# A fused attention and feed-forward kernel on one core: the last batch's norm writes token order, and the last output tile is summed in two column pieces

## The chip, the cores and the metric

The kernel runs on one core of one Trainium2 chip. The metric is the device time of one execution in microseconds (us), the median of several runs. The engines are named as the profile names them: PE is the matrix engine (PEld its weight loads), DVE the vector engine, ACT the scalar engine, POOL the GpSimd engine and SP the engine that here only issues DMAs. "hT", "A", "o" and the like are names of tiles in the program; "L601" is line 601 of the kernel.

## The reference, cut to what matters

```python
# q, k, v: (8 batches, 8 heads, 576 tokens, 64); p: (8, 8, 32, 64), all float32
def sm_attn(qq, kk, vv):
    s = scale * np.matmul(qq, kk.transpose(0, 1, 3, 2))      # scale = 1/8
    a = np.exp(s - np.max(s, axis=-1, keepdims=True))
    a = a / (np.sum(a, axis=-1, keepdims=True) + 1e-09)
    return np.matmul(a, vv)
p_packed = sm_attn(p, k, v)                # 32 packed rows per head
out = sm_attn(q, p_packed, p_packed)       # (8, 8, 576, 64)
x = out.transpose(0, 2, 1, 3).reshape(4608, 512)
h = x @ w_in                               # (4608, 2048)
g = np.where(h >= 1, h, np.where(h <= -1, 0.0, (h + 1) ** 2 / 4))
return g @ w_out                           # (4608, 512) float32
```

## The kernel before

**Tiling.** The work goes batch by batch, 8 batches of 576 tokens. For a batch, K and Q are turned so that the head dimension lies on the partitions, the packed attention gives `ppT`, and two things follow from it: `M = ppT · w_in` (the packed rows already sent through the first weights; 128 partitions by 2 head groups `g` by 2048), and the second softmax `A` (128 partitions by 2 groups `g`, two halves `x` of 288 tokens each). `A` is made by a chain: exponentials `eT` on ACT, their sums `sm` on PE, `ln` and `rc = exp(-ln)` on ACT, and then `norm` (L473) on DVE, which multiplies `eT` by the packed rows' reciprocal `rs` and by `rc`. There are two norms for a batch, one for each group.

**Hidden tiles.** `hidden_tile` makes one of 16 blocks `fi` of 128 hidden units of a batch: four matmuls (L549: group 0 with halves 0 and 1, then group 1 with halves 0 and 1) into a PSUM tile `h`, then `x` on ACT (L554), a second step on DVE or ACT (L559, L561) and a third on DVE (L564) that writes the block into `hT`. With `M` and `A` both in, the block needs all four halves of `A`.

**Output tiles.** Two batches make a pair of 1152 token columns in `hT`, and nine output tiles of 128 columns each. `out_tile` sums 16 matmuls (L601) of 512 columns in a PSUM tile `o`, copies it to `ob` (L320 is the line of the copying helper, on ACT or DVE), and SP issues the DMAs that write the rows to the output. Token columns don't stand in the order of the output's rows: half `x` holds three stretches `e` of 96 columns, and column `t` of stretch `e` is row `6t + 2e + x` of the batch. So a tile's rows are written in pieces that end at each 96th column, two for most tiles. In the last pair, tiles 0 to 3 need batch 6 alone, tile 4 both, and tiles 5 to 8 batch 7.

**The last tile** (pair 3, tile 8) is summed in two halves of 256 columns, one in `o`, one in a PSUM tile `o2` of the pool `psW`. For each `fi` PE runs both halves, one after the other. At the end ACT copies columns 0 to 255 and issues two DMAs of its own (96 and 32 rows), DVE copies columns 256 to 511, and SP issues two DMAs for these.

**What sets the order.** Everything is given to a planner (`Plan`) as tasks with dependencies, keys and costs `C[...]`; it simulates the engines and writes each engine's instructions in the order in which it would start them. A changed cost can therefore move instructions on PE, ACT and DVE. PE's instruction stream takes an output matmul wherever the hidden tiles leave room. The DMAs of ACT and SP count their landing in eight counters, DMAHW0 to DMAHW7, which DMAs take in turn; a DMA waits for the one before it on its counter. Behind the program's last instruction SP waits for all of the counters, one after the other, in the order of their numbers (the instructions at L702).

Of the kernel before, what the change touches and what calls it, by code (L numbers as in the profile page):

```python
# [8 lines left out]

C = dict(load=3.5666, half=1.46, w_in=2.57, w_out=2.57, rest=1.25, out=9, p=4.05, land=2.0125, xt=6.5, xland=11, tpp=0.06, tp=0.042, sc=0.034, pk=0.9765, s2=0.2862, sm=0.245, M=0.2415, h=0.49, o=0.217, switch=0.05, join=0.1604, pTc=0.1, Tca=1.12, Tcd=0.76, ex=0.82, ppT=0.42, ppo=0.41, ppa=0.4, ppd=0.2, rs=0.18, eT=0.74, ln=0.65, rc=0.68, A=0.82, Mca=1, Mcd=1.22, x=0.65, ta=0.683, td=0.489, hT=0.758, oba=0.585, obd=0.6276, array=0.2, wake=1.2, warm=4.2, early=0.3, tell=0.034, feed=0.085, slack=0.51, margin=0.1717, wait=0.5)
NW, NO, NX, NB = 3, 2, 5, 6
DW, FILL = 256, 512
TURNED = 3


# [164 lines left out]
def kernel(  # L182
# [10 lines left out]
    nc = tc.nc  # L193
# [44 lines left out]
    def wide(shape, dtype, name):  # L238
        return psW.tile(shape, dtype, tag="w", name=name)
# [61 lines left out]
    add_weights("in", 0)  # L301
    add_weights("in", 1)
    add_weights("out", 0)
    add_weights("in", 2)
    add_weights("out", 1)
    add_weights("in", 3)
    add_weights("out", 2)
    add_load("k", 1, 2)
    add_load("v", 1, 1)
    add_load("q", 1, 2)  # L310
    add_weights("out", 3)
    L["p"] = add(DMA, C["rest"], -1, (), lambda: nc.gpsimd.dma_start(p_nat[:, PB * 2:], p_v[:, PB * 2:]))


# [4 lines left out]
    def copy(out_, in_):  # L319
        return lambda eng: nc.vector.tensor_copy(out_, in_) if eng == DVE else nc.scalar.copy(out_, in_)  # L320
# [37 lines left out]
    def attention(b, key):  # L358
# [85 lines left out]
        def weights(g, deps, r):  # L444
# [25 lines left out]
                nc.scalar.activation(box["rc"], box["ln"], AF.Exp, scale=-1.0)  # L470

            def norm(eng):
                nc.vector.scalar_tensor_tensor(A()[:, g], box["eT"], rs()[:, g, :1], box["rc"], ALU.mult, ALU.mult)  # L473
            p_ = K.get((b - 1, "A" + str(g)), [])
            t, j = yield ky, C["s2"], deps + p_, mm
# [50 lines left out]
        pk, pc, r = zip(*([packed((0,), [e0]), packed((1,), [e1])] if b == 0 else [packed((0, 1), [e0, e1])] * G))  # L526
# [58 lines left out]
    def out_tile(pr, i):  # L585
        box, prev = {}, []
        bs = range(2 * pr + i * P // S, 2 * pr + ((i + 1) * P - 1) // S + 1)

        end = 2 * pr + 2 == B and i + 1 == NT

        cuts = [12, KF] if pr == 0 and i < 4 else [KF]
        w = d_model // 2

        def spare():
            box["o2"] = wide([P, w], f32, "o2")

        def step(fi):
            if fi == 0 or fi in cuts:
                box["o"] = psO.tile([P, d_model], f32, tag="o", name="o")
            for o, cs in [(box["o"][:, :w], slice(w)), (box["o2"], slice(w, d_model))] if end else [(box["o"], slice(d_model))]:  # L600
                nc.tensor.matmul(o, hT[:, fi, i * P:(i + 1) * P], w_out_sb[:, fi, cs], start=(fi == 0 or fi in cuts), stop=(fi + 1 in cuts))  # L601

        def kept(eng):
            box["part"] = att.tile([P, d_model], f32, tag="part", name="part", bufs=4)
            copy(box["part"], box["o"])(eng)

        def done(eng):
            box["ob"] = ops.tile([P, d_model], f32, tag="ob", name="ob")
            if len(cuts) > 1:
                nc.vector.tensor_tensor(box["ob"], box["o"], box["part"], ALU.add)  # L610
            else:
                copy(box["ob"], box["o"])(eng)
            for a, n, dst in out_rows(pr, i):
                nc.sync.dma_start(dst, box["ob"][a:a + n])

        def done_last(eng):

            for j, (eng, queue, o) in enumerate(((ACT, nc.scalar, box["o"][:, :w]), (DVE, nc.sync, box["o2"]))):
                ob = ops.tile([P, w], f32, tag="ob" + str(j), name="ob" + str(j), bufs=1)
                copy(ob, o)(eng)  # L620
                for a, n, dst in sorted(out_rows(pr, i), key=lambda x: -x[1]):
                    queue.dma_start(dst[:, j * w:(j + 1) * w], ob[a:a + n])
        if end:
            prev = [add(PE, 0.0, 100 + pr * NT + i, [K[B - 1, "h"][-1]], spare, takes="W", readers=1)]
        for fi in range(KF):
            t = add(PE, C["o"], 100 + pr * NT + i, [wrote[b, fi] for b in bs] + prev + [L["out", fi // 4]],
                    lambda fi=fi: step(fi), mode=0, takes="O" if fi == 0 or fi in cuts else None, readers=1, slack=C["slack"])
            step_of[pr, i, fi] = t
            prev = [t]
            if fi == 0 or fi in cuts:  # L630
                owner = t
            if fi + 1 in cuts[:-1]:
                first = both(kept, C["oba"], C["obd"], b_key(pr, i), prev, frees=owner)
        if len(cuts) > 1:
            add(DVE, C["obd"], b_key(pr, i), prev + [first], done, frees=owner, takes="ob", holds=C["out"])
        else:
            both(done_last if end else done, C["oba"], C["obd"], b_key(pr, i), prev, frees=owner, takes="ob", holds=C["out"])

    def b_key(pr, i):
        return -0.5  # L640
# [10 lines left out]
    keys = {0: {nm: -1 + 0.01 * i for i, nm in enumerate(names)}}  # L651
    for f in range(1, NF):
        keys[0]["M" + str(f)] = 0.25 * f - 0.12
    order = "kT0 kT1 sc0 qT0 sc1 qT1 pk0 s20 M0 s21 sm0 M1 sm1 M2 M3".split()
    for b in range(1, B):
        lo, hi = (b - 1 + 0.05, b - 0.05)
# [50 lines left out]
```

## Time and profile before

| what | value |
|---|---|
| median of 3 runs | 250.54 us (250.51 to 250.75) |
| the profiled execution's own time | 249.87 us |
| its span, first to last instruction | 247.8 us |
| granted clock, mean | 0.997 |
| PE busy | 237.5 us, 96% |
| ACT busy, DVE busy | 186.2 us (75%), 180.7 us (73%) |
| L601, the output matmuls, on PE | 144.5 us |
| L549, the hidden matmuls, on PE | 75.1 us |

The span runs from the first to the last instruction; the time of an execution is 2.1 us longer. Rows of a timeline give start, duration, engine, line and tile; a bracket at a row's end says how long the engine was idle before it, and who ended that. A group's row gives count, busy time and the mean duration of one.

### The profile page before, as it was taken

How to read it: one execution, taken by the hardware profiler on the slowest of the kernel's cores; microseconds unless marked ns; L12 is line 12 of the kernel's file. 1: busy time of each engine (PE TensorE's matmuls, PEld its weight loads, DVE VectorE, ACT ScalarE, POOL GpSimd, SP SyncE). 2: the span in 40 equal slices, each digit the busy share in tenths (PEclk: the TensorE clock that was granted, in tenths of full speed). 3: DMA queues.
4: the chain of work that ended last, by engine and by line, in shares of the span. 5: the costliest groups of instructions: out<-in, count | busy, mean ns of one | idle time of the engine just before them, and what ended most of it. 6: DMA issues, size and time to landing. Idle time of an engine off the chain costs nothing.

```text
span 247.8 us, 5398 instructions
## 1 busy us (share of the span) xinstructions
PE 237.5 (96%) x2191; PEld 137.5 (55%) x2191; DVE 180.7 (73%) x312; ACT 186.2 (75%) x294; POOL 29.3 (12%) x44
## 2 busy tenths in 40 slices
PE   7879899999989999999999999999999999999993
PEld 2545466467636744665456644665466546654452
DVE  5455998889997987798859884799579967992000
ACT  3358895899889998698769888698888886982110
POOL 8632331212001030011001100000000000000000
PEclk9999999999999999999999999999999999999998
DMA  6999999999999999879998984641571121112223
GB/s 100 201 207 207 206 203 196 203 221 257 167 191 154 237 205 222 193 108 171 151 171 141 163 166 93 138 93 38 95 93 42 33 54 44 45 42 85 56 74 85
DMA packets 54825, 34.37 MB, mean 139 GB/s; under 512 B 27536, under 2 KB 50320, under 8 KB 54800
## 3 DMA queue, kind: packets, MB, share of 16 engines
q0 software_dynamic: 24672, 18.55, 50.0%
q1 hardware_dynamic: 29968, 15.34, 31.9%
q8 instruction: 17, 0.28, 0.5%
q10 hardware_dynamic: 160, 0.13, 0.2%
q14 instruction: 8, 0.07, 0.1%
HBM read 37.22 MB, written 9.44 MB: 188 GB/s over the span
## 4 chain that ended last, share of the span: by engine, by line
PE 79%; DMA 10%; DVE 6%; ACT 2%; issue 1%; POOL 1%; ACTq 0%; POOLq 0%
PE o L601 47%; PE h L549 21%; DMA w_in_sb<-in_moe_w_in_dram 8%; PE mp L494 3%; DVE hT L564 3%; DMA k<-in_k_dram 3%; PE pk L418 2%; PE sp L398 2%; PE tp L377 2%; PE sm L462 1%; DVE x L559 1%; PE s L452 1%; PE pk L424 1%; DVE pT L320 1%; ACT rc L470 1%
## 5 line engine op out<-in xcount | busy, mean ns | idle before, releaser
L601 PE MATMUL o<-w_out_sb,hT 128*128 128x512 bf16 (+1 forms) x592 | 144.5, 374 | 0.7 <-DVE hT L564 0.6
L564 DVE SCALAR_TENSOR_TENSOR hT<-x 128x576 bf16<-128x576 f32 x128 | 94.5, 755 | 5.4 <-ACT x L561 2.6
L554 ACT ACTIVATE x<-h 128x576 f32<-128x576 f32 x128 | 77.8, 656 | 12.6 <-PE h L549 9.9
L601 PEld LDWEIGHTS <-hT 128*128 128x128 bf16 x592 | 55.8, 98 | 55.7 <-issue 5.8
L549 PE MATMUL h<-A,M 128*128 128x288 bf16 x512 | 75.1, 286 | 0.5 <-ACT M L320 0.5
L549 PEld LDWEIGHTS <-M 128*128 128x128 bf16 x512 | 49.5, 98 | 21.5 <-issue 1.1
L559 DVE TENSOR_SCALAR x<-x 128x576 f32<-128x576 f32 x87 | 39.9, 458 | 11.0 <-ACT x L554 11.0
L561 ACT ACTIVATE x<-x 128x576 f32<-128x576 f32 x41 | 27.2, 683 | 0.1
L320 ACT COPY ob<-o 128x512 f32<-128x512 f32 (+1 forms) x19 | 10.9, 575 | 19.4 <-PE o L601 19.3
L320 DVE COPY ob<-o 128x512 f32<-128x512 f32 (+1 forms) x14 | 9.4, 668 | 22.0 <-PE o L601 22.0
L320 ACT CAST M<-mp 128x1024 bf16<-128x1024 f32 x22 | 21.3, 1019 | 3.2 <-PE mp L494 3.2
L473 DVE SCALAR_TENSOR_TENSOR A<-eT,rs,rc 128x576 bf16<-128x576 bf16 x16 | 13.0, 814 | 6.1 <-ACT rc L470 6.1
L320 DVE CAST M<-mp 128x1024 bf16<-128x1024 f32 x10 | 12.1, 1220 | 6.4 <-PE mp L494 6.4
L401 ACT ACTIVATE ex<-sp 96x768 bf16<-96x768 f32 x16 | 13.0, 813 | 4.4 <-PE sp L398 4.3
L457 ACT ACTIVATE eT<-s,rs 128x576 bf16<-128x576 f32 x16 | 11.3, 740 | 4.7 <-PE s L452 4.7
L466 ACT ACTIVATE ln<-sm 128x576 f32<-128x576 f32 x16 | 10.4, 651 | 3.8 <-PE sm L462 3.4
L260 POOL DMA_DIRECT2D q<-in_q_dram x10 | 7.4, 744 | 47.6 <-DMA qT<-q 33.3
L494 PE MATMUL mp<-w_in_sb,ppT 64*32 64x512 bf16 x256 | 10.5, 380 | 2.3 <-DMA w_in_sb<-in_moe_w_in_dram 2.2
L260 POOL DMA_DIRECT2D k<-in_k_dram x10 | 7.5, 753 | 44.1 <-DMA kT<-k 27.5
L676 PE MATMUL o<-zeros 128*128 128x512 bf16 (+1 forms) x39 | 10.8, 406 | 1.2 <-DVE zeros L248 1.2
L470 ACT ACTIVATE rc<-ln 128x576 f32<-128x576 f32 x16 | 10.9, 683 | 0.5
L398 PEld LDWEIGHTS <-kT 128*128 128x128 bf16 x192 | 7.6, 98 | 2.8 <-DVE kT L320 1.0
(50 smaller groups left out, 117.2 us busy)
## 6 DMA issues: line engine op xcount, KB each, us to landing
out_dram<-ob SPq DMA_DIRECT2D x23, 192.0 KB, 2.8
v<-in_v_dram POOLq DMA_DIRECT2D x7, 576.0 KB, 18.3
k<-in_k_dram POOLq DMA_DIRECT2D x6, 576.0 KB, 12.4
q<-in_q_dram POOLq DMA_DIRECT2D x6, 576.0 KB, 12.1
out_dram<-ob SPq DMA_DIRECT2D x24, 128.0 KB, 2.9
w_in_sb<-in_moe_w_in_dram POOLq DMA_DIRECT2D x4, 512.0 KB, 14.6
w_out_sb<-in_moe_w_out_dram POOLq DMA_DIRECT2D x4, 512.0 KB, 16.9
out_dram<-ob SPq DMA_DIRECT2D x23, 64.0 KB, 2.0
```

Source lines behind the costliest of these rows:

```text
L260: nc.gpsimd.dma_start(tok[nm, b][:, hs].rearrange("p h c d -> p h (c d)"), SRC[nm][b, hs].rearrange("h (p c) d -> p h (c d)", c=NC))
L320: return lambda eng: nc.vector.tensor_copy(out_, in_) if eng == DVE else nc.scalar.copy(out_, in_)
L401: nc.scalar.activation(ex()[:, :, i].rearrange("p e x a n -> p e (x a n)"), box["sp"], AF.Exp, scale=scale)
L470: nc.scalar.activation(box["rc"], box["ln"], AF.Exp, scale=-1.0)
L473: nc.vector.scalar_tensor_tensor(A()[:, g], box["eT"], rs()[:, g, :1], box["rc"], ALU.mult, ALU.mult)
L494: nc.tensor.matmul(mp[a * NP:(a + 1) * NP, g], pp_of(y, h), w_in_sb[y * D:(y + 1) * D, h // 2, f * FW:(f + 1) * FW], start=True, stop=True)
L549: nc.tensor.matmul(h[:, hf, :HALF], T[b, "M"][:, g, fi * P:(fi + 1) * P], T[b, "A"][:, g, hf], start=(g == 0), stop=(g == G - 1))
L554: nc.scalar.activation(box["x"], box["h"][:, :, :HALF], AF.Prelu, bias=-1.0, alpha=0.5)
L559: nc.vector.tensor_scalar(x, x, 1.0, 0.0, ALU.add, ALU.max)
L561: nc.scalar.activation(x, x, AF.Relu, bias=1.0)
L564: nc.vector.scalar_tensor_tensor(hT[:, fi, col:col + S].rearrange("p (a t) -> p a t", a=2), box["x"], 1.0, box["x"], ALU.min, ALU.mult)
L601: nc.tensor.matmul(o, hT[:, fi, i * P:(i + 1) * P], w_out_sb[:, fi, cs], start=(fi == 0 or fi in cuts), stop=(fi + 1 in cuts))
```

## The change

The change has five edits. Two of them move instructions on the chip; the planner's answer to them is a third.

1. **Token order.** For the last batch (batch 7), `norm` is issued as two instructions of 288 columns, one for each half, which read `eT` and `rc` with a step of 96 elements between neighbours and write `A` with column `3t + e`, the order of the output's rows. `out_rows` follows: a tile's rows of that batch are one DMA for each half that it touches. The planner's cost of the batch's norm grows by 0.28.
2. **Last tile by columns.** The last tile sums columns 0 to 383 over all 16 `fi` first, in `o`, then columns 384 to 511 over all 16, in a wide tile of `psW`. DVE copies the first piece and SP issues its DMA; ACT copies the second and issues its DMA.
3. **The key list** for batches 1 to 7 has one more entry (`pk1`).
4. The loads of batch 1 are written as a string `ORDER`, in the order that they had.
5. `PARTS`, `CUT`, `klo` and `khi` name numbers that stood in the code (4, 12, 0.05 and 0.05).

```diff
-    order = "kT0 kT1 sc0 qT0 sc1 qT1 pk0 s20 M0 s21 sm0 M1 sm1 M2 M3".split()
+    order = "kT0 kT1 sc0 qT0 sc1 qT1 pk0 pk1 s20 M0 s21 sm0 M1 sm1 M2 M3".split()
...
             def norm(eng):
+                if b == B - 1:
+                    for x in range(X):
+                        o, e, r_ = [v.rearrange(w, e=E) for v, w in ((A()[:, g, x], "p (t e) -> p t e"),
+                                    (box["eT"][:, x], "p (e t) -> p t e"), (box["rc"][:, x], "p (e t) -> p t e"))]
+                        nc.vector.scalar_tensor_tensor(o, e, rs()[:, g, :1], r_, ALU.mult, ALU.mult)
+                    return
                 nc.vector.scalar_tensor_tensor(A()[:, g], box["eT"], rs()[:, g, :1], box["rc"], ALU.mult, ALU.mult)
...
-            a_ = add(DVE, C["A"], km, [i_] + K.get((b - 2, "h"), []), norm)
+            a_ = add(DVE, C["A"] + (0.28 if b == B - 1 else 0.0), km, [i_] + K.get((b - 2, "h"), []), norm)
...
+            if b == B - 1:
+                r = t % HALF
+                n = min(HALF - r, (i + 1) * P - t)
+                res.append((t - i * P, n, out[b * S:(b + 1) * S].rearrange("(r x) d -> x r d", x=X)[x, r:r + n]))
+                t += n
+                continue
...
+        pieces = [slice(0, 3 * d_model // 4), slice(3 * d_model // 4, d_model)] if end else [slice(0, d_model)]
...
-            for a, n, dst in out_rows(pr, i):
-                nc.sync.dma_start(dst, box["ob"][a:a + n])
-
-        def done_last(eng):
-
-            for j, (eng, queue, o) in enumerate(((ACT, nc.scalar, box["o"][:, :w]), (DVE, nc.sync, box["o2"]))):
-                ob = ops.tile([P, w], f32, tag="ob" + str(j), name="ob" + str(j), bufs=1)
-                copy(ob, o)(eng)
-                for a, n, dst in sorted(out_rows(pr, i), key=lambda x: -x[1]):
-                    queue.dma_start(dst[:, j * w:(j + 1) * w], ob[a:a + n])
...
+                (nc.scalar if j else nc.sync).dma_start(dst[:, cs], ob[a:a + n])
+        for j, cs in enumerate(pieces):
+            cost = C["o"] * (cs.stop - cs.start) / d_model
+            if j:
+                prev = prev + [add(PE, 0.0, 100 + pr * NT + i, prev, lambda: room(1), takes="W", readers=1)]
+                owner = prev[-1]
+            for fi in range(KF):
+                t = add(PE, cost, 100 + pr * NT + i, [wrote[b, fi] for b in bs] + prev + [L["out", fi // 4]],
+                        lambda fi=fi, j=j, cs=cs: step(fi, j, cs), mode=0, takes="O" if not j and (fi == 0 or fi in cuts) else None,
+                        readers=1, slack=C["slack"])
...
+            elif end:
+                add(ACT if j else DVE, C["oba"] if j else C["obd"], b_key(pr, i), prev, fn,
+                    frees=owner, takes="ob", holds=C["out"])
```

Up to the norms of batch 7 every engine's instructions are in the order that they had. What moves behind that point is shown at three places. The first is DVE at batch 7's norms, just ahead of its first hidden tile (A is the norms' output, ob a copy of an output tile of batch 6, x and hT steps of the hidden tiles). Before:

```order
L473 SCALAR_TENSOR_TENSOR A<-eT,rs,rc 128x576
L320 COPY ob<-o 128x512
L473 SCALAR_TENSOR_TENSOR A<-eT,rs,rc 128x576
L559 TENSOR_SCALAR x<-x 128x576
L564 SCALAR_TENSOR_TENSOR hT<-x 128x576
```

and in the changed kernel, whose lines have other numbers:

```order
L483 SCALAR_TENSOR_TENSOR A<-eT,rs,rc 128x288 x2
L325 COPY ob<-o 128x512
L483 SCALAR_TENSOR_TENSOR A<-eT,rs,rc 128x288 x2
L571 TENSOR_SCALAR x<-x 128x576
L576 SCALAR_TENSOR_TENSOR hT<-x 128x576
```

Each norm is two instructions of half the width; the copy between the two norms stays where it was. Further on, one copy of an output tile goes from ACT to DVE.

The second place is PE where batch 7's hidden tiles begin (o is an output tile of batch 6, h the first hidden tile; a bracket names the engine whose counter an instruction waits for). Before, the last output matmuls and the first hidden tile:

```order
L601 LDWEIGHTS hT [waits DVE_49]
L601 MATMUL o<-w_out_sb,hT 128x512
L549 LDWEIGHTS M [waits DVE_49]
L549 MATMUL h<-A,M 128x288 [waits PE_49]
L549 LDWEIGHTS M
L549 MATMUL h<-A,M 128x288
L549 LDWEIGHTS M
L549 MATMUL h<-A,M 128x288 [waits DVE_49]
L549 LDWEIGHTS M
L549 MATMUL h<-A,M 128x288
```

In the changed kernel 18 output matmuls stand ahead of the first hidden tile, where 16 stood; the last one of them and the hidden tile are:

```order
L619 LDWEIGHTS hT [waits DVE_49]
L619 MATMUL o<-w_out_sb,hT 128x512
L561 LDWEIGHTS M [waits DVE_49]
L561 MATMUL h<-A,M 128x288 [waits PE_49]
L561 LDWEIGHTS M
L561 MATMUL h<-A,M 128x288 [waits DVE_49]
L561 LDWEIGHTS M
L561 MATMUL h<-A,M 128x288 [waits DVE_49]
L561 LDWEIGHTS M
L561 MATMUL h<-A,M 128x288 [waits DVE_49]
```

Each of the four matmuls now waits for its own half of A. Two output matmuls have moved ahead of the hidden tiles and a third between them, so that 130 output matmuls stand behind the last hidden tile instead of 133.

The third place is the program's end on SP and ACT (ob is the copied output tile; DMAHW names the counter whose earlier DMA must have landed). SP before:

```order
L614 DMA out_dram<-ob 96x512 [waits DMAHW7_49,Activation_49]
L614 DMA out_dram<-ob 32x512 [waits DMAHW0_49]
L614 DMA out_dram<-ob 64x512 [waits DMAHW1_49,Activation_49]
L614 DMA out_dram<-ob 64x512 [waits DMAHW2_49]
L622 DMA out_dram<-ob_3588 96x256 [waits DMAHW4_49,DVE_49]
L622 DMA out_dram<-ob_3588 32x256 [waits DMAHW6_49]
```

ACT before:

```order
L320 COPY ob<-o 128x512 [waits DMAHW4_49,DMAHW3_49,PE_49]
L320 COPY ob<-o 128x512 [waits DMAHW6_49,DMAHW5_49,PE_49]
L320 COPY ob_3584<-o 128x256 [waits PE_49]
L622 DMA out_dram<-ob_3584 96x256 [waits DMAHW3_49,Activation_49]
L622 DMA out_dram<-ob_3584 32x256 [waits DMAHW5_49]
```

SP in the changed kernel:

```order
L634 DMA out_dram<-ob 128x512 [waits DMAHW5_49,Activation_49]
L634 DMA out_dram<-ob 96x512 [waits DMAHW6_49,Activation_49]
L634 DMA out_dram<-ob 32x512 [waits DMAHW7_49]
L634 DMA out_dram<-ob 128x512 [waits DMAHW0_49,Activation_49]
L634 DMA out_dram<-ob 128x384 [waits DMAHW1_49,DVE_49]
```

ACT in the changed kernel:

```order
L325 COPY ob<-o 128x512 [waits DMAHW2_49,DMAHW1_49,PE_49]
L325 COPY ob<-o 128x512 [waits DMAHW4_49,DMAHW3_49,PE_49]
L325 COPY ob<-o 128x512 [waits DMAHW6_49,DMAHW5_49,PE_49]
L325 COPY ob<-o_3567 128x128 [waits DMAHW1_49,DMAHW2_49,PE_49,Activation_49]
L634 DMA out_dram<-ob 128x128 [waits Activation_49]
```

The last four DMAs took counters 3 to 6. In the changed kernel the last two take counters 1 (SP's 128x384) and 2 (ACT's 128x128), since the tiles of batch 7 need fewer DMAs.

More of the change, by code (lines that the diff above doesn't have):

```diff
@@ L589, in out_tile @@
         end = 2 * pr + 2 == B and i + 1 == NT
[L591 to L601, printed above, removed]
@@ L603, in kept, with room @@
-        def kept(eng):
[L604 to L608, printed above, removed]
+        cuts = [CUT, KF] if pr == 0 and i < PARTS else [KF]
+        pieces = [slice(0, 3 * d_model // 4), slice(3 * d_model // 4, d_model)] if end else [slice(0, d_model)]
+        def room(j):
+            box["o", j] = wide([P, d_model], f32, "o2") if j else psO.tile([P, d_model], f32, tag="o", name="o")
@@ new lines, in step, with done @@
+        def step(fi, j, cs):
+            if not j and (fi == 0 or fi in cuts):
+                room(0)
+            nc.tensor.matmul(box["o", j][:, :cs.stop - cs.start], hT[:, fi, i * P:(i + 1) * P], w_out_sb[:, fi, cs],
+                             start=(fi == 0 or fi in cuts), stop=(fi + 1 in cuts))
+        def kept(eng):
+            box["part"] = att.tile([P, d_model], f32, tag="part", name="part", bufs=PARTS)
+            copy(box["part"], box["o", 0])(eng)
+        def done(eng, j, cs):
+            ob, o = ops.tile([P, d_model], f32, tag="ob", name="ob"), box["o", j]
+            ob, o = [v[:, :cs.stop - cs.start] for v in (ob, o)]
@@ L623, in out_tile @@
[L623 to L637, printed above, removed]
+                (nc.scalar if j else nc.sync).dma_start(dst[:, cs], ob[a:a + n])
[8 more added lines that the diff above has]
+                        readers=1, slack=C["slack"])
+                if not j:
+                    step_of[pr, i, fi] = t
+                prev = [t]
+                if t.takes:
+                    owner = t
+                if fi + 1 in cuts[:-1]:
+                    first = both(kept, C["oba"], C["obd"], b_key(pr, i), prev, frees=owner)
+            fn = lambda eng, j=j, cs=cs: done(eng, j, cs)
+            if len(cuts) > 1:
+                add(DVE, C["obd"], b_key(pr, i), prev + [first], fn, frees=owner, takes="ob", holds=C["out"])
+            elif end:
+                add(ACT if j else DVE, C["oba"] if j else C["obd"], b_key(pr, i), prev, fn,
+                    frees=owner, takes="ob", holds=C["out"])
+            else:
+                both(fn, C["oba"], C["obd"], b_key(pr, i), prev, frees=owner, takes="ob", holds=C["out"])
```

36 lines of the change are left out of this document (20 added, 16 removed).

## The prediction

> **What bounds the kernel now.** I read the page first, for the busy shares and the chain that ended last.
>
> ```profile
> span 247.8 us, 5398 instructions
> PE 237.5 (96%) x2191; PEld 137.5 (55%) x2191; DVE 180.7 (73%) x312; ACT 186.2 (75%) x294; POOL 29.3 (12%) x44
> PE 79%; DMA 10%; DVE 6%; ACT 2%; issue 1%; POOL 1%; ACTq 0%; POOLq 0%
> ```
>
> PE is busy for 96% of the span and carries 79% of the chain. A share over the whole span doesn't say where the change can act, so next I cut the end of the program, the only part in which instructions move, into stretches.
>
> ```profile
> core 0: us, PE busy (x) PEld busy (x) DVE busy (x) ACT busy (x) POOL busy (x), PEclk, DMA share, GB/s
> 203.00:218.00 15.00, 15.00 (x98) 9.46 (x97) 11.99 (x20) 12.40 (x21) 0.00 (x0) 1.00 0.15 41
> 218.00:243.60 25.60, 25.60 (x138) 13.21 (x136) 5.87 (x9) 8.33 (x15) 0.00 (x0) 1.00 0.29 72
> 243.60:247.80 4.20, 0.26 (x3) 0.00 (x0) 0.42 (x1) 0.37 (x1) 0.00 (x0) 0.84 0.21 62
> ```
>
> From 203.0 to 243.6 PE is busy all the time, at the full granted clock. In the first stretch, the hidden tiles of batch 7, DVE and ACT have 3.0 and 2.6 us left out of 15. In the second they are mostly idle. The last stretch is 4.2 us in which PE has nothing left: a copy, the last DMAs and the program's end. Two things follow. Nothing can be won on PE, whose columns the change does not make fewer; a wait of PE would be paid in full. And what can be won lies in those 4.2 us.
>
> **The norms of batch 7.** The timeline there:
>
> ```profile
> 203.44 3.62 PE L601 MATMUL o<-w_out_sb,hT 128*128 128x512 bf16 x16
> 204.36 0.82 DVE L473 SCALAR_TENSOR_TENSOR A<-eT,rs,rc 128x576 bf16<-128x576 bf16 x1 [0.91 <-ACT rc L470]
> 205.09 0.68 DVE L320 COPY ob<-o 128x512 f32<-128x512 f32 x1
> 205.76 0.82 DVE L473 SCALAR_TENSOR_TENSOR A<-eT,rs,rc 128x576 bf16<-128x576 bf16 x1
> 206.89 2.12 PE L549 MATMUL h<-A,M 128*128 128x288 bf16 x16
> L601 PE MATMUL o<-w_out_sb,hT 128*128 128x512 bf16 x174 | 40.5, 379 | 0.0
> L549 PE MATMUL h<-A,M 128*128 128x288 bf16 x88 | 13.1, 286 | 0.0
> 71.91 0.77 DVE hT L564
> 72.73 0.39 PE o L601
> ```
>
> The second norm ends at 206.58. PE starts the first hidden tile at 206.89, straight behind 16 output matmuls. The two groups' rows give a single matmul's duration, 0.38 and 0.29 us, which overlaps the next one's. The last two rows, from the chain, are a place where PE did wait for DVE: DVE's end at 72.68 let PE start at 72.73, so a wait costs 0.05 us beyond the end itself.
>
> To cost a half norm I need DVE's price for a column and for an instruction; the groups kept apart by shape give it.
>
> ```profile
> L320 DVE COPY ob<-o 128x512 f32<-128x512 f32 x13 | 8.9, 687 | 3.2 <-PE o L601 3.2
> L320 DVE COPY ob<-o 128x256 f32<-128x256 f32 x1 | 0.4, 424 | 18.8 <-PE o L601 18.8
> L473 DVE SCALAR_TENSOR_TENSOR A<-eT,rs,rc 128x576 bf16<-128x576 bf16 x16 | 13.0, 814 | 6.1 <-ACT rc L470 6.1
> ```
>
> 256 more columns cost 263 ns, 1.03 ns each. At that rate 593 of a norm's 814 ns are columns and 221 are the instruction's own. A norm of 288 columns is then 221 + 297 = 518 ns, and a pair 1.04 us, 0.22 more than before. For two groups the second norm ends 0.44 us later, at 207.02.
>
> The cover is in the order: two more output matmuls stand ahead of the first hidden tile. One takes (3.62 - 0.38) / 15 = 0.216 us, so PE gets there at 206.89 + 0.43 = 207.32. Only the tile's fourth matmul needs the last half, and three matmuls at (2.12 - 0.29) / 15 = 0.122 us come before it: 207.69. With the 0.05 us from above, the norms may end as late as 207.64, which is 1.06 us later than before. 0.44 of it is used and 0.62 left. I cost this edit at nothing; from 1.06 us on, each further microsecond is paid by PE in full.
>
> What no row shows is a read with a step of 96 elements; every DVE row here reads neighbours. From below it could cost what neighbours cost; a gain is excluded, since DVE's earlier end releases nothing that PE isn't already filling. From above I take twice the time for a column: 221 + 593 = 814 ns for a half, 0.81 us more for a pair, 1.62 us for two, and PE waits 1.62 - 1.06 = 0.56 us. I take the lower value, since all rows to be had are at it, and keep the upper for the range.
>
> The Trainium skill speaks against the step: "SBUF — State Buffer", section "Door 1: The DMA port swizzle", says that accesses which leave a 16-byte line each time pay a penalty, and both inputs leave theirs at each step; no run here shows it, and it gives no figure. Without a figure it picks no value between those ends.
>
> **What comes later for it.** The hidden tiles start 0.43 us later, and DVE takes over one copy of 0.69 us from ACT. Their last block ends here:
>
> ```profile
> 224.33 0.76 DVE L564 SCALAR_TENSOR_TENSOR hT<-x 128x576 bf16<-128x576 f32 x1 [0.82 <-ACT x L561]
> ```
>
> At 225.09, then, and with both additions at 226.2. The first output tile that needs batch 7 has 4 × 16 matmuls of 512 columns and the last tile's 3.5 us behind its start: it starts at about 243.7 - 3.5 - 13.8 = 226.4 and needs its sixteenth block 15 × 0.216 = 3.2 us later. That covers it. For the same reason the copy's move costs nothing: DVE has 3.0 us free in the hidden tiles' stretch. The loads' string, the named numbers and the key list change no order ahead of the norms: nothing.
>
> **PE in the last tile.** 16 times 384 + 128 columns instead of 16 times 256 + 256.
>
> ```profile
> 243.04 0.82 PE L601 MATMUL o<-w_out_sb,hT 128*128 128x256 bf16 x6
> L601 PE MATMUL o<-w_out_sb,hT 128*128 128x256 bf16 x32 | 3.7, 272 | 0.0
> 36.31 0.35 PE sp L398 x12
> 36.15 0.51 PE L398 MATMUL sp<-pT,kT 128*128 128x64 bf16 x12
> L601 PEld LDWEIGHTS <-hT 128*128 128x128 bf16 x592 | 55.8, 98 | 55.7 <-issue 5.8
> ```
>
> A matmul of 256 columns takes (0.82 - 0.27) / 5 = 0.109 us, half of 0.216, so the time goes by columns: 0.162 for 384 and 0.055 for 128, the same sum. Each has a weight load of its own. A load is busy for 98 ns, but 12 matmuls of 64 columns, each with its own load of the same size, took 0.35 us, 29 ns each; so loads overlap well below 55 ns. PE's end doesn't move.
>
> Here too the Trainium skill is less kind: "TensorE: Matmul & The Clock Gate", section "Back-to-back issue gap", gives about 81 ns a matmul as the sustained rate at 128 columns with its load. By that the second piece would take 16 × 26 ns = 0.42 us longer; the trace's 29 ns at 64 columns does not agree. By the 81 ns the whole would come to 250.67 us.
>
> **The tail.** The last 4 us in detail: the copies, the issues in the timeline with a window on the last of them, each DMA's time to landing (short windows of the DMA view), and SP's last waits.
>
> ```profile
> 243.78 0.37 ACT L320 COPY ob<-o 128x256 f32<-128x256 f32 x1 [2.80 <-PE o L601]
> 243.89 0.42 DVE L320 COPY ob<-o 128x256 f32<-128x256 f32 x1 [18.80 <-PE o L601]
> 244.19 0.86 ACTq L622 DMA_DIRECT2D out_dram<-ob  x2
> 244.72 0.42 SPq L622 DMA_DIRECT2D out_dram<-ob  x1
> out_dram<-ob SPq DMA_DIRECT2D x1, 32.0 KB, 2.1
> L702 SPq EVENT_SEMAPHORE  x4: 28/28/28, 245.2 to 245.4; - x4
> L702 SPq EVENT_SEMAPHORE  x2: 27/28/28, 246.8 to 246.9; - x2
> ```
>
> Before, the last DMA is SP's second, 32 rows: issued at 244.72, landed 2.1 us later at 246.8. SP's waits for the counters then end: counter 6 at 246.8, counter 7 at 246.9. Where nothing holds them, such waits stand (245.4 - 245.2) / 3 = 0.067 us apart.
>
> After: PE is done when it was, so ACT starts its copy of 128 columns at 243.89. Its price and the landing times of DMAs that flow alone in the last 25 us:
>
> ```profile
> L320 ACT COPY p<-pk 64x128 f32<-64x128 f32 x2 | 0.5, 263 | 1.8 <-PE pk L424 1.8
> out_dram<-ob SPq DMA_DIRECT2D x1, 64.0 KB, 1.6
> out_dram<-ob SPq DMA_DIRECT2D x1, 192.0 KB, 2.3
> out_dram<-ob SPq DMA_DIRECT2D x2, 128.0 KB, 2.3
> out_dram<-ob SPq DMA_DIRECT2D x1, 128.0 KB, 2.4
> ```
>
> The copy ends at 243.89 + 0.26 = 244.15 and the issue follows 0.04 us later, as ACT's did before (243.78 + 0.37 to 244.19): 244.19. This one DMA is 64 KB in 128 rows. Of the same bytes, 32 rows landed in 1.6 us; of the rows nearest in number, 64 (128 KB), landed in 2.3 and 2.4. I take 2.05, the middle: it has the bytes of the one and more rows than the other. It lands at 246.24, 0.56 us earlier than the last one before.
>
> SP's piece is earlier: its sum ends 16 × 0.055 = 0.89 us before PE's end, DVE starts at 243.00, copies 384 columns in 0.42 + 128 × 1.03 ns = 0.56 us, and SP issues at about 243.60; 192 KB lands 2.3 us later, at 245.9. It is not last.
>
> But the end moves the other way at the counters. The last DMA had counter 6, with one counter behind it. Now it has counter 2, and SP still goes through 3 to 7: four waits more, 4 × 0.067 = 0.27 us, although all of them have long been met.
>
> **The sum.** -0.56 + 0.27 = -0.29 us, norms and PE at nothing. The profiled execution's 249.87 us would be 249.58; that execution was 0.67 us shorter than the median of the runs, and I carry the difference over: 250.54 - 0.29 = 250.25 us. A difference of 0.2% (0.5 us) is about what a measurement of this kernel can tell from no change, and this gain is smaller.
>
> **The rivals.**
>
> *The last DMA lands faster.* At 1.6 us, ACT's DMA lands at 245.79, and SP's at 245.89 is the last, with counter 1 and five waits more than before (0.33): -0.91 + 0.33 = -0.58 us, 249.96. For it speaks the row of equal bytes, against it the rows of 64.
>
> *No gain at all.* At 2.4 us it lands at 246.59: -0.21 + 0.27 = +0.06 us, 250.60. Then the two shorter queues only pay for the longer walk through the counters. That ACT had a queue of its own before as well speaks for this: the second queue is not new, only one DMA for each.
>
> *The step of 96 is slow, and PE waits: slower.* The place is the first hidden tile's third and fourth matmuls. It decides from 1.06 us for two norms, a half norm of 675 ns or 1.58 ns for a column, and shows as a slowdown of over 0.2% from another 0.8 us on. At twice the price the time is 250.25 + 0.56 = 250.81. At three times a half takes 1.11 us, two pairs 2.8 us more, and PE waits 1.74 us: 251.99. By the Trainium skill's rule on 16-byte lines (the section named above) some of this would come, how much it doesn't say.
>
> *Weight loads bound the narrow matmuls: slower.* If a load's 98 ns were the step, the second piece would take 16 × 43 ns = 0.68 us longer: 250.93. Against it stand the 29 ns.
>
> **How the numbers follow.** The forecast (landing in between, norms covered) has 0.55, the fast landing 0.23, no gain 0.07, slow reads 0.11 (0.03 of it below twice the price, which stays within 0.2%), weight loads 0.04. So faster by over 0.2%: 0.23; within: 0.55 + 0.07 + 0.03 = 0.65; slower: 0.08 + 0.04 = 0.12. The range goes from the fast landing's 249.96, with a little for the spread of the runs, 249.9, to twice the price for reads, 250.8; that leaves out the slowest reads and the weight loads.
>
> **What would show it.** Right: two rows of 128x288 on DVE of about 0.52 us each, no idle time of PE ahead of its hidden tiles, PE ending at the same time in the span, ACT's last DMA landing about 2.05 us after its issue, and six SP waits in a row behind that landing. Wrong: an idle gap of PE released by DVE's A; the second piece's matmuls further apart than 0.06 us; a landing outside 1.6 to 2.4 us; the span changing by over 0.6 us either way.

## The result, and the profile after

The changed kernel takes 249.26 us (median of 6 runs, 248.87 to 249.70); the kernel before, in turn with it, took 250.41 us. The ratio is 0.9966, 95% interval [0.9952, 0.9979]: 0.85 us faster, between 0.5 and 1.2; the two medians by themselves are 1.15 us apart. The forecast was 250.25 us and 0.29 us faster, with a range that ended at 249.9: too small a gain.

The profiled execution happens to have the same span as that of before, 247.8 us (its time is 249.70, against 249.87), although the medians differ. So the two were laid side by side by stretches. The same three windows as in the prediction:

```profile
core 0: us, PE busy (x) PEld busy (x) DVE busy (x) ACT busy (x) POOL busy (x), PEclk, DMA share, GB/s
203.00:218.00 15.00, 14.90 (x95) 9.34 (x96) 11.85 (x21) 11.68 (x20) 0.00 (x0) 1.00 0.19 50
218.00:243.60 25.60, 25.49 (x128) 12.39 (x128) 7.66 (x13) 8.94 (x16) 0.00 (x0) 1.00 0.26 72
243.60:247.80 4.20, 0.91 (x17) 0.73 (x14) 0.56 (x1) 0.27 (x1) 0.00 (x0) 1.00 0.19 62
```

PE is still full up to the last stretch, and its 0.91 us there (0.26 before) say that everything in this execution is some 0.65 us later. Where that comes from is far ahead of the change; the timelines, first of before, then of after, where the fourth block of `M` starts:

```profile
29.70 0.41 PE L494 MATMUL mp<-w_in_sb,ppT 64*32 64x512 bf16 x8 [0.60 <-DMA w_in_sb<-in_moe_w_in_dram]
```

```profile
30.38 0.41 PE L506 MATMUL mp<-w_in_sb,ppT 64*32 64x512 bf16 x8 [1.17 <-DMA w_in_sb<-in_moe_w_in_dram]
```

PE waits for a load of `w_in`, which landed 0.68 us later in this execution. Over the profiles of the experiments below this start lies anywhere from 29.55 to 31.01 us, whatever the kernel, and from it to the last batch's norms the time was the same to within 0.2 us. The changed kernel has three profiles, with this start at 29.94, 30.38 and 31.01 us; from it to the end of the span all three take 217.4 us. So the start is chance, and it makes the spread of these three. The comparison of the changed part has to be made from a point behind it.

The norms of batch 7 (timeline, then the groups by shape):

```profile
204.31 3.83 PE L619 MATMUL o<-w_out_sb,hT 128*128 128x512 bf16 x17
205.01 1.01 DVE L483 SCALAR_TENSOR_TENSOR A<-eT,rs,rc 128x288 bf16<-128x288 bf16 x2 [0.91 <-ACT rc L475]
206.54 0.99 DVE L483 SCALAR_TENSOR_TENSOR A<-eT,rs,rc 128x288 bf16<-128x288 bf16 x2
207.98 2.12 PE L561 MATMUL h<-A,M 128*128 128x288 bf16 x16
L483 DVE SCALAR_TENSOR_TENSOR A<-eT,rs,rc 128x288 bf16<-128x288 bf16 x4 | 2.0, 539 | 0.9 <-ACT rc L475 0.9
L619 PE MATMUL o<-w_out_sb,hT 128*128 128x128 bf16 x16 | 1.1, 219 | 0.0
```

The norms end at 207.53, PE starts its first hidden tile at 207.98 straight from the output matmuls, with no bracket of idle time. From the first norm's start to the end of PE's last matmul it is 39.50 us in both traces: PE's end has not moved. The last row is the last tile's second piece: the starts of its matmuls are 0.056 us apart in the trace; (1.1 - 0.22) / 15 gives that within the row's rounding.

The tail: copies and issue in the timeline, landings in short windows of the DMA view, then SP's last waits.

```profile
243.65 0.56 DVE L325 COPY ob<-o 128x384 f32<-128x384 f32 x1 [17.24 <-DMA out_dram<-ob]
244.59 0.27 ACT L325 COPY ob<-o 128x128 f32<-128x128 f32 x1 [2.95 <-PE o L619]
244.88 0.38 ACTq L634 DMA_DIRECT2D out_dram<-ob  x1
out_dram<-ob SPq DMA_DIRECT2D x1, 192.0 KB, 1.9
out_dram<-ob ACTq DMA_DIRECT2D x1, 64.0 KB, 1.7
L723 SPq EVENT_SEMAPHORE  x1: 28/28/28, 246.2 to 246.2; - x1
L723 SPq EVENT_SEMAPHORE  x6: 28/28/28, 246.6 to 246.9; - x6
```

ACT's DMA lands 1.69 us behind its issue, at 246.58, not after 2.05. Then six waits follow in a row, 0.061 us apart. From the start of the last copy to the end of the span it is 3.87 us before (243.89 to 247.76) and 3.21 after (244.59 to 247.80): 0.66 us less, and 0.62 less counted from the end of PE's last matmul (3.91 before, 3.29 after), behind which the last copy now starts 0.04 us later. That is the change's work inside the span. The rest of the gain is outside it: an execution's time is longer than its span by 2.11 us before (96 runs, 2.05 to 2.17) and by 1.91 after (23 runs, 1.86 to 1.97). Three executions of the kernel before that took 350 to 861 us are left out of all means.

Taken over these runs (those of the experiments included), the mean goes from 250.27 to 249.39, 0.88 us: 0.68 in the span, of which 0.62 is what lies behind PE's end and the small rest within what the start varies, and 0.20 outside it.

### The profile page after: what moved, and what is told of

Read it like the earlier page. It is cut to its first block, busy times and chain, and to the rows that moved or that the text cites. A ratio compares the mean times of both kernels' runs of the same rounds, so it can differ in the third digit from the quotient of the medians.

```text
span 247.8 us, 5367 instructions
## 1 busy us (share of the span) xinstructions
PE 235.8 (95%) x2156; PEld 137.5 (55%) x2191; DVE 181.9 (73%) x315; ACT 185.6 (75%) x293; POOL 29.1 (12%) x44
## 4 chain that ended last, share of the span: by engine, by line
PE 76%; DMA 11%; DVE 6%; ACT 3%; issue 2%; POOL 1%; ACTq 0%; POOLq 0%
PE o L619 45%; PE h L561 20%; DMA w_in_sb<-in_moe_w_in_dram 8%; DVE hT L576 3%; DMA k<-in_k_dram 3%; PE mp L506 3%; PE pk L423 2%; PE sp L403 2%; PE tp L382 1%; DVE x L571 1%; PE sm L467 1%; PE s L457 1%; PE pk L429 1%; DVE ob L630 1%; ACT rc L475 1%
## 5 line engine op out<-in xcount | busy, mean ns | idle before, releaser
L619 PE MATMUL o<-w_out_sb,hT 128*128 128x512 bf16 (+2 forms) x559 | 136.0, 373 | 2.4 <-issue 0.8
L619 PEld LDWEIGHTS <-hT 128*128 128x128 bf16 x592 | 55.2, 98 | 56.3 <-issue 5.8
L325 DVE COPY ob<-o 128x512 f32<-128x512 f32 (+1 forms) x15 | 10.2, 677 | 20.5 <-DMA out_dram<-ob 17.2
L325 ACT COPY ob<-o 128x512 f32<-128x512 f32 (+1 forms) x18 | 10.2, 568 | 19.5 <-PE o L619 19.3
L485 DVE SCALAR_TENSOR_TENSOR A<-eT,rs,rc 128x576 bf16<-128x576 bf16 x14 | 11.4, 813 | 5.1 <-ACT rc L475 5.1
L697 PE MATMUL o<-zeros 128*128 128x512 bf16 (+1 forms) x37 | 11.5, 442 | 1.5 <-DVE zeros L256 1.2
```

The costliest lines, as they stand in the source:

```text
L619: nc.tensor.matmul(box["o", j][:, :cs.stop - cs.start], hT[:, fi, i * P:(i + 1) * P], w_out_sb[:, fi, cs], start=(fi == 0 or fi in cuts), ...
```

## The experiments

Below, "tail" is the time from the start of the last copy to the end of the span (3.87 us before, 3.21 after), and "outside" the time of an execution beyond its span. The theory after the result was: the tail is shorter because the end hangs on one DMA of 64 KB that lands in 1.7 us; the norms are covered. Its rivals: the gain belongs to one of the two parts alone, to the second queue, or to the counters.

**Each part alone.** Before with the token order and nothing else; and after without it:

```diff
 e1_tokens (before, with the norm in halves and out_rows by halves)
+                if b == B - 1:
+                    for x in range(X):
...
 e2_columns (after)
-                if b == B - 1:
+                if b == B:
...
-            if b == B - 1:
+            if b == B:
```

> The kernel before with the token order of batch 7 alone (two half norms, one DMA for each half and piece); the last tile is still summed in two interleaved halves of 256 columns. Theory 'tail' (all of the gain lies between the last copy and the end, because few and whole DMAs land sooner): two DMAs of 128 rows and 128 KB in place of four; the later is issued at about 0.45 us behind the last copy's start as before's first ones were, lands about 1.9 us on, and five counters follow it (0.30 us): from the last copy's start to the end of the span 3.4 to 3.6 us, where before has 3.87 and the changed kernel 3.21; the time falls by 0.3 to 0.45 us. PE has no idle time released by A. Rival 'columns' (the gain comes from the earlier first piece): no gain, 3.8 to 4.0 us, since the walk through the counters (+0.24) eats what the merged DMAs bring. Rival 'order elsewhere' (the token order saves time ahead of the tail): the time falls by 0.6 us or more while the tail is 3.6 us or longer.

> The kernel before with the last tile by columns alone (0 to 383, then 384 to 511); batch 7 keeps its column order and its one-instruction norms, so each queue issues two DMAs (32 rows, then 96). Theory 'tail': ACT's second DMA is issued about 0.4 us behind its first, so the last landing is about 0.4 us later than in the changed kernel, but only one counter follows it (counter 6, as before): 3.21 + 0.4 - 0.24 = 3.4 us from the last copy's start to the end; the time falls by 0.4 to 0.5 us. Rival 'whole DMAs alone bring it': the tail stays within 0.1 us of before's 3.87.

The token order alone took 249.84 us against 250.22 (ratio 0.9986 [0.9971, 1.0]) with a tail of 3.82; the columns alone took 249.74 (0.9989 [0.9978, 1.0001]) with 3.53. For the first the tail theory missed: the time fell by as much as it said, but by luck, for the tail stayed where the rival 'columns' had it. Its two last DMAs in the DMA view:

```profile
out_dram<-ob ACTq DMA_DIRECT2D x1, 128.0 KB, 1.9
out_dram<-ob SPq DMA_DIRECT2D x1, 128.0 KB, 2.1
```

ACT issues at 244.36 and SP at 244.52; the later one lands after 2.13 us, with five counters still behind it. With fewer DMAs, but both at nearly the same moment and early in the counters, nothing is left of the gain in the tail. What is faster lies outside the span: 1.77 us in place of 2.11. The columns alone leave two DMAs on each queue; ACT's second is issued at 245.60, 0.42 behind the first, and lands last. Outside the span this kernel has 1.79 us, so part of its gain, too, isn't the tail's. Neither part has the whole gain: the tail's gains are 0.05 and 0.34 alone, 0.66 together. The token order makes it one DMA a queue, the columns set the two apart in time.

**The norms.** Each half norm issued twice, and half norms that read neighbours in place of every 96th element:

```diff
 e4_norm_twice (after)
-                    for x in range(X):
+                    for x in [0, 1, 0, 1]:
 e11_neighbours (after)
-                                    (box["eT"][:, x], "p (e t) -> p t e"), (box["rc"][:, x], "p (e t) -> p t e"))]
+                                    (box["eT"][:, x], "p (t e) -> p t e"), (box["rc"][:, x], "p (t e) -> p t e"))]
```

> The changed kernel with each half norm of batch 7 issued twice (same values written again; the planner's costs are the same, so the order is). It prices the cover of the norms. In the changed kernel's trace the second pair ends 207.54 with PE 0.65 us later than in the trace before, so 206.89 on the old scale, 0.75 us ahead of 207.64, the latest harmless time. Two pairs more cost 2 x 0.95 = 1.9 us. Theory 'covered': PE idles 1.9 - 0.75 = 1.1 to 1.2 us ahead of the first hidden tile's later matmuls, and the time grows by about that. Rival 'norms off the path': no idle time of PE, no change. Rival 'no cover': 1.9 us.

> The changed kernel, whose half norms read eT and rc as neighbours, without the step of 96 elements; so the columns of batch 7 go to rows that aren't theirs. In the changed kernel a half norm took 0.53 to 0.55 us. Theory 'a step costs nothing': 0.53 to 0.55 us again. Rival 'a step costs something that the prediction's price hid': 0.52 us or less, the prediction's figure for neighbours.

With the norms twice the kernel took 250.82 us (1.0029 [1.0015, 1.0043]), PE's end came 1.1 us later, and the tail stayed at 3.18. Timeline and group:

```profile
209.04 0.28 PE L561 MATMUL h<-A,M 128*128 128x288 bf16 x1 [0.58 <-DVE A L483]
209.49 0.77 PE L561 MATMUL h<-A,M 128*128 128x288 bf16 x5 [0.17 <-DVE A L483]
L561 PE MATMUL h<-A,M 128*128 128x288 bf16 x512 | 75.5, 286 | 2.1 <-DVE A L483 0.8 <-ACT M L325 0.5 <-issue 0.2
```

Now PE waits for `A` at the third and fourth matmul, which is where the prediction had put it. At 0.122 us a matmul the third would start at 208.29; it starts 0.75 us later, and the fourth loses 0.33 more, together 1.08, near the 1.1 to 1.2 that was expected. (The brackets are shorter, for they count from the end of the matmul before.) In the changed kernel itself the norms end in time. Against the mean of after the time grew by 1.5 us; the 0.4 beyond the trace's 1.1 are not in this stretch, and no run settles whether they are the starts of these five runs. With neighbours, the row of the groups is:

```profile
L483 DVE SCALAR_TENSOR_TENSOR A<-eT,rs,rc 128x288 bf16<-128x288 bf16 x4 | 1.9, 513 | 0.9 <-ACT rc L475 0.9
```

513 ns against 539: the step of 96 costs 0.03 us a half norm, 0.1 us over the four, under cover. The single run of this kernel took 249.24 us, as after did.

**The queue and the counters.** SP issues the second piece as well; tiles 5 and 6 in pieces of at most 32 rows, so that more DMAs come before and the last one takes counter 7; and both together:

```diff
 e6_one_queue, e9_one_queue_counter7 (after)
-                (nc.scalar if j else nc.sync).dma_start(dst[:, cs], ob[a:a + n])
+                nc.sync.dma_start(dst[:, cs], ob[a:a + n])
 e3_counters, e9_one_queue_counter7 (after)
-                n = min(HALF - r, (i + 1) * P - t)
+                n = min(HALF - r, (i + 1) * P - t, 32 if i in (5, 6) else P)
```

> The changed kernel, but SP issues the second piece's DMA too, behind ACT's copy. SP is free again 0.65 us before the copy ends. Theory 'the second queue is worth nothing here': SP issues at the same time within 0.05 us, lands the same 1.70 us later; tail 3.2 us, no change. Rival 'a queue of its own lets the second piece pass the first': the landing comes 0.2 us or more later, behind the 192 KB of the first piece, tail 3.4 us or more.

> The changed kernel, but the rows of output tiles 5 and 6 of the last pair are written in pieces of at most 32 rows: five DMAs more, all ahead of tile 7, so that ACT's last DMA takes counter 7 instead of 2 and no counter is left behind it. Theory (SP walks through the counters one by one, 0.06 us each, also through those long met): the end comes 0.31 us sooner behind the same landing, 2.9 us from the last copy's start instead of 3.21, and the time falls by 0.3 us against the changed kernel. Rival (the waits for met counters run beside something that ends at the same time, or the extra DMAs delay the last landing): 3.2 us, no change.

> The changed kernel with both edits that shortened its tail: tiles 5 and 6 written in pieces of at most 32 rows, so that the last DMA takes counter 7, and SP issues the last tile's second piece too (it landed 1.63 us after issue from SP, 1.67 to 1.70 from ACT). Theory: the two add up, -0.33 and -0.06 us: a tail of 2.82 us from the last copy's start; 0.35 to 0.4 us faster than the changed kernel, about 1.0 us (0.4%) faster than the kernel before. Rival: the extra DMAs on SP's queue, of which the last tile's now are two more, make the last one land later (1.9 us): a tail of 3.0 us or more.

| kernel | time, us (before) | ratio | tail | outside |
|---|---|---|---|---|
| e6_one_queue | 249.14 (250.27) | 0.9960 [0.9946, 0.9974] | 3.15 | 1.76 |
| e3_counters | 249.54 (250.22) | 0.9973 [0.9963, 0.9982] | 2.87 | 2.12 |
| e9_one_queue_counter7 | 248.72 (250.75) | 0.9935 [0.9911, 0.9959] | 2.82 | 1.77 |

The second queue brings nothing: with 0.6 us between the two issues, one queue takes both, and its DMA lands in 1.63 us. The counters' walk is real: with the last DMA on counter 7, the other waits are over before it lands. The last landing and SP's waits in the last kernel (the third wait of the last row comes behind the counters):

```profile
out_dram<-ob SPq DMA_DIRECT2D x1, 64.0 KB, 1.6
L723 SPq EVENT_SEMAPHORE  x7: 27/28/28, 244.7 to 245.1; - x7
L723 SPq EVENT_SEMAPHORE  x3: 17/28/28, 245.7 to 246.2; - x3
```

The tail came out as expected, 0.33 and 0.39 us shorter than in after. But e3's time, forecast 0.3 us below after's, is no better than it: its time outside the span went up by 0.2, and the 0.1 that should be left is less than the starts vary. With both edits that time is low again, and the kernel beats both: 248.72 us, where after took 249.42 among the same runs. Of these 0.70 us the tail explains 0.38 and the time outside 0.14; the rest is not explained by either.

**When a DMA lands.** The cut elsewhere in the last tile, and tile 5 in DMAs of 64 rows:

```diff
 e7_half_half: slice(0, 256), slice(256, d_model); e8_eighth: slice(0, 448), slice(448, d_model)
 e12_rows64 (after)
-                n = min(HALF - r, (i + 1) * P - t)
+                n = min(HALF - r, (i + 1) * P - t, 64 if i == 5 else P)
```

> The changed kernel with the pieces cut at column 256 in place of 384: ACT's last DMA has 128 KB in 128 rows of 1 KB, its copy is 256 columns wide (0.372 us in place of 0.265). Theory 'bytes in flight set the landing': 0.2 to 0.4 us more than 1.70, since twice the bytes have to flow and the first piece's DMA, issued later as well, still flows; with the copy's 0.11 the tail is 3.5 to 3.7 us. Rival 'rows set it' (the number of rows decides, as the prediction's middle value half assumed): 1.70 us again, and a tail of 3.31 us.

> The changed kernel with the pieces cut at column 448: ACT's last DMA has 32 KB in 128 rows of 256 bytes, its copy is 64 columns wide (about 0.21 us). PE: 16 matmuls of 64 columns, at the 29 ns of the score matmuls. Theory 'bytes set the landing': 1.55 to 1.65 us, with the copy's 0.05 us a tail of 3.05 to 3.1 us, unless SP's 224 KB, issued only about 0.2 us ahead, becomes the last one to land. Rival 'rows or small packets set it': 1.70 us or more, no gain: a tail of 3.2 us or longer.

> The changed kernel with tile 5 of the last pair (128 rows of 2 KB, one DMA, with nothing else in flight) written in two DMAs of 64 rows. Theory 'a DMA of 64 rows is slow for its number of rows, and the prediction's upper value (2.3 to 2.4 us) came from that': the first of the two is issued in 0.47 us and lands 2.3 us after its issue, later than 128 rows with the same 128 KB (1.91) or with twice as much. Rival 'those 64-row DMAs were slow for the place that they write': 0.35 us and 1.9 us. The tail is the changed kernel's, 3.2 us, less one counter (0.06).

The half cut took 249.69 (0.9977 [0.9969, 0.9986]) with a tail of 3.54, as expected. The eighth took 250.18 (0.9995 [0.998, 1.001]) with 3.67, where 3.05 to 3.1 was expected. Their last DMAs in the DMA view, e7 first, then e8:

```profile
out_dram<-ob ACTq DMA_DIRECT2D x1, 128.0 KB, 1.9
```

```profile
out_dram<-ob SPq DMA_DIRECT2D x1, 224.0 KB, 2.1
out_dram<-ob ACTq DMA_DIRECT2D x1, 32.0 KB, 2.2
```

128 KB in 128 rows land in 1.9 us. The 32 KB in e8, issued 0.1 us behind 224 KB, take 2.2: the smaller DMA landed later than the larger one of after. The likely cause is that it was issued on top of another, as in e1, where 128 KB issued 0.16 us behind another DMA took 2.13 in place of 1.91. Its short rows of 256 bytes are a rival that no run sets apart. So the place of the cut looks like a balance of size and distance, and of those tried three quarters was best. And tile 5, first in e12 as two DMAs of 64 rows, then in after as one of 128:

```profile
out_dram<-ob SPq DMA_DIRECT2D x2, 128.0 KB, 2.3
out_dram<-ob SPq DMA_DIRECT2D x1, 256.0 KB, 2.0
```

Half of the rows and bytes land later, after 2.25 and 2.40 us against 2.03. DMAs like these gave the prediction its upper end. In e12 they are a pair again, the second issued 0.52 us behind the first, and no run issues 64 rows alone. But the first one's issue took 0.47 us against 0.36 and was over before the second began, so that much is its own. The one run of e12 took 249.32 us, with a tail of 3.12.

**Repeats of after** took 249.35 (0.9967 [0.9956, 0.9979]) and 249.42 (0.9955 [0.9938, 0.9971]), with tails of 3.20 and 3.19.

> The changed kernel once more, beside the next three. In six profiles so far the stretch from the matmuls of the fourth block of M (29.7 to 30.7 us) to the norms of batch 7 has the same length within 0.03 us, and all of the difference between the changed kernel and the one before that is left lies behind PE's end: -0.62 us. Theory 'tail and chance': with more runs the difference is -0.5 to -0.7 us, a ratio of 0.997 to 0.998, and the six first runs' -0.85 us had some luck in it. Rival 'something ahead of the tail': it stays at -0.85 us or more, with a fixed stretch that is shorter than before's.

> The changed kernel a third time, on the same chip as the kernel above. By its tail the difference from before is -0.62 us, a ratio of 0.9975; the two measurements so far said 0.9966 and 0.9967, with intervals that reach 0.9979. Theory 'chance of the start': the fixed stretch from the fourth block of M to batch 7's norms is 173.25 us again, the tail 3.2 us, and the ratio falls anywhere from 0.996 to 0.998. Rival 'a gain ahead of the tail': again 0.9967 or less, with starts that are earlier than before's on the whole.

Of both, the theory 'tail and chance' gave too small a gain, and the rival's earlier gain isn't in the traces: up to the norms they are as long as before's to within 0.03 us. What was missing lies outside the span.

**The time outside the span.** It is the same in every run of a kernel to about 0.06 us (spans are on record to 0.1 us), and differs between kernels. Up to here it went with the number of instructions in ACT's program (waits and registers included): 439 in e1, e6, e9 (1.76 to 1.77), 440 in after, e4, e7, e8 (1.90 to 1.92), 441 in before, e3, e12 (2.10 to 2.12), 443 in e2 (1.79). (The kept traces show two instructions fewer in each.) These kernels differ in more, so the last four change little beside the count, by copies done twice where nothing waits; the first has two copies more and one of ACT's other instructions less:

```diff
 e13_act441: (5, 6); e14_act442: (5, 6, 7); e15_act443: (3, 5, 6, 7); e16_act444: (3, 4, 5, 6, 7)
                 copy(ob, o)(eng)
+                if pr == 3 and i in (5, 6):
+                    copy(ob, o)(eng)
```

> After, with the copies of the output tiles 5 and 6 done twice, so that ACT's program has one instruction more: 441 instead of 440, as many as before the change. PE is not waiting for these copies, so the span should stay (last copy's start to the end 3.2 us). Theory 'count' (the time outside the span goes by the number of ACT's instructions, in steps of four): 2.10 us outside the span instead of 1.91, so 0.19 us slower than after. Rival 'noise or another cause' (the level belongs to something else of the kernel): 1.91 as in after.

> The same with the tiles 5, 6 and 7 copied twice: 442 instructions on ACT. No kernel so far had this remainder of four, so theory 'count' says only that the time outside the span is that of one of its levels, 1.77 to 2.15 us, and the same in every run to 0.06. Rival: 1.91.

> The same with the tiles 3, 5, 6 and 7 copied twice: 443 instructions on ACT. Theory 'count': 1.77 to 1.79 us outside the span, 0.13 less than after with three instructions more. A theory by which each more instruction costs a little: more than 2.10. Rival: 1.91.

> The same with the tiles 3 to 7 copied twice: 444 instructions on ACT. Theory 'count' in steps of four: 1.91 us again, as after with 440. Rival 'any other rule by the count': another level.

| ACT's instructions | 440 (after) | 441 | 442 | 443 | 444 |
|---|---|---|---|---|---|
| outside, mean us | 1.91 | 2.12 | 1.90 | 1.79 | 1.84 |
| tail, us | 3.21 | 3.21 | 3.19 | 3.21 | 3.20 |
| time, us (before 250.08) | - | 249.33 | 249.49 | 248.91 | 249.33 |

At 441 instructions the 0.2 us are back, and at 443 the time is 0.33 us below that, both as expected, with the tail unchanged: as far as these kernels go, this time follows the count. That it repeats in steps of four is not borne out (444 has 1.84, not 1.91). Why a count should do this stays open; the trace shows nothing outside the span.

## Why the prediction was wrong, and where it was right

**The landing of the last DMA was the step that failed.** The prediction took 2.05 us, the middle between 1.6 (the same bytes in 32 rows) and 2.3 to 2.4 (64 rows). Measured were 1.69 us in after, 1.67 and 1.68 in its repeats, 1.63 and 1.59 from SP. So the row of equal bytes was near, and the 64-row DMAs, taken as nearest in number of rows, were not: e12 has them slower than 128 rows of the same tile. Nor did the rows that the prediction calls alone stand alone: the 64-row DMAs were pairs 0.52 us apart, and the 192 KB of 2.3 us stood 0.37 us behind the 64 KB. The term is -0.92 us, not -0.56. That is the rival of the fast landing, which had 0.23, in the tail within a tenth of a microsecond (-0.58 forecast, -0.66 measured). But that rival had SP's 192 KB land last, after 2.3 us; they landed in 1.94, ahead of ACT's.

**The time outside the span was taken as unchanged,** without saying so, when the difference in the span was put onto the median. It fell by 0.20 us. Nothing in the profile of before could have given that number, but two kernels' times and spans would have shown that it isn't a constant. With the landing as measured the forecast would have been 249.89, at the lower end of the range; the 0.20 make it 249.69, and the kernel before was at 250.41 here and not at 250.54, which makes it 249.56. The 0.3 us that are left to 249.26 are put down to chance of the six runs: their medians differ by 1.15 us, the means over all runs by 0.88.

**The walk through the counters** was right: +0.27 predicted, +0.24 measured, four waits of 0.061 (-0.92 and it make -0.68, and the tail shows -0.66). e3 and e9 took the walk away and got 0.33 and 0.39 us for it and for a landing that was 0.04 and 0.10 us shorter.

**The norms at nothing** were right. A half took 0.54 us where 0.518 was forecast, and the last norm ended 0.30 us later than before (counted from the first norm's start), not 0.44. Reading neighbours, a half took 0.513 us (e11), so the step costs 0.03 us, far from the doubled price for a column that the range allowed for. With the Trainium skill's rule on leaving 16-byte lines ("SBUF — State Buffer", section "Door 1: The DMA port swizzle") the trace agrees in sign. e4 shows that the cover has an end, at the matmuls named.

**PE's columns at nothing** were right: 0.056 us a matmul of 128 columns, 0.055 forecast. The 81 ns of the Trainium skill ("TensorE: Matmul & The Clock Gate", section "Back-to-back issue gap") don't hold here; the measurement decides.

**Two queues** were credited with nothing of their own in the sum, and e6 bears that out: what helped is one DMA for each piece and time between the pieces.

## What to carry to other kernels

At the end of a program, count the last DMA's landing, what was issued within 0.2 us of it, and the waits behind it on counters that have long been met: a DMA alone and on the last counter was worth 1 us here (tail 3.87 to 2.82). Price a landing from a DMA of the same bytes and the same number of rows, with nothing beside it, or keep both ends as likely. And before a difference of 0.2 us is explained inside the span, look at time minus span for both kernels.

## What the runs showed of the hardware that was not expected

- DMAs of 64 rows of 2 KB, issued as a pair, landed in 2.25 and 2.40 us (e12), one of 128 rows of 2 KB in 2.02 (after), 32 rows in 1.62 to 1.75 (e3); issuing the second 64-row DMA took 0.59 us against 0.35 for 128 rows.
- Of two DMAs issued 0.1 to 0.16 us apart on two queues, the later landed after 2.13 us (e1, 128 KB) and 2.21 (e8, 32 KB); 128 KB issued 1.7 us behind another landed in 1.91 (e7).
- The time of an execution outside its span goes up and down between 1.77 and 2.12 us with the number of ACT's instructions, and one instruction can be worth 0.2 us.
- A load that PE waits for once, near the start, lets it go on at 29.55 to 31.01 us, and all that follows moves with it: in three profiles of one kernel by 1.07 us, and the span with it.
